# A planned attention and gated-MLP kernel: the planner groups matmuls by array mode, weight narrowing is spread differently, and the last block's first feature tile is cut in two

## The chip, the cores and the metric

The kernel runs on one NeuronCore of a Trainium2 chip. The metric is device time in microseconds (us) of one execution, with all loads from and stores to HBM. Five engines work side by side, each through its own instructions in order: PE (TensorE, matrix products; its weight loads are listed as PEld), DVE (VectorE), ACT (ScalarE), POOL (GpSimd) and SP (SyncE, which here issues the transfers).

## What is computed

Performer attention over 8 batches x 8 heads x 576 tokens x 64, with 128 random features, then RMS norm and a gated MLP on all 4608 tokens (512 to 1536 to 512). Cut to the core:

```python
def phi(x):                                   # x: q or k, scaled by 64 ** -0.25
    proj = einsum('bhsd,md->bhsm', x, omega)  # 128 features
    h = proj - sum(x * x, -1) / 2
    return exp(h - max(h, -1)) / sqrt(m)
kv, z = einsum('bhsm,bhsd->bhmd', phi(k), v), phi(k).sum(2)
num, den = einsum('bhsm,bhmd->bhsd', phi(q), kv), einsum('bhsm,bhm->bhs', phi(q), z) + 1e-6
x = (num / den) as 4608 x 512
xn = x / sqrt(mean(x * x) + 1e-6) * rms_g
g = xn @ w_gate                               # 512 x 1536, float64
out = (g * sigmoid(g) * (xn @ w_val)) @ w_out # 1536 x 512, float64
```

The three weight matrices come in as float64 and are narrowed to float32 on the chip.

## The kernel before

**Tiling.** Tokens go in 36 chunks of 128, and four chunks make a block of 512 columns (9 blocks). A product of float32 operands is made of three passes: each operand is held as a high part and a remainder, and `three_pass` multiplies high by high (L209), high by remainder (L210) and remainder by high (L211).

**Phase one** (0 to 453.6 us in the profile) makes the attention and the first 4 of the 12 feature tiles of the MLP, f0 to f3. For each chunk of k and of q, `project` (L512, a bank of pool psJ) multiplies 64 rows of the array per head, `peak` takes maxima on DVE (L525), `exps` runs on ACT (L542). `kv_mid` (L601) and `kv_half` (L640) sum keys against values, 64 columns of the array at a time. For each chunk `attend` then transposes the q features (`turn`, L673, matmuls with the identity), multiplies them with kv (`mix`, L684, 64 columns of the array), divides (`divide`, DVE L698 to L700), scales (L722), transposes (`xturn`, L734), copies to `xr` and to the high part (ACT, L740 and L750), takes the remainder on POOL (`xlo`, L753) and stores (`xstore`, L743). When the four chunks of a block are done, `gated` multiplies each feature tile: 12 matmuls of 512 columns for the gate and 12 for the value, each into a bank of pool psF (2 banks), then ACT L808, DVE L812 and L818, and the store L823. Until the first of these, the planner fills PE's idle time with `spin` (L840), a matmul of 512 columns with no use for its result.

**Phase two** (453.6 to 805 us) makes the other 8 feature tiles by products of the Strassen-Winograd kind: in each of two passes (PASSES, two tile pairs each), 5 pairs of blocks by 4 units (a unit is gate or value of a tile pair), a unit being 7 products of 6 matmuls. The products go to bank `a` (pool psJ), `b` (psM) and `c` (psF). Between them ACT copies bank contents out (`keep`, L1047) and DVE adds them (`total`, L1054). The seventh product (on Rt4) accumulates into bank `a` again, so it starts only when `total` c22 on DVE has read it. The left operands of the products (`left`, lw_0 to lw_6) are loaded and split by ACT L900 and POOL L905, the right ones (`right`, Xb loads L944) by DVE and ACT, once for a pair of blocks.

**Phase three** (805 us to the end) is the product with w_out.

**Narrowing.** `weights(n)` narrows one of 36 weight tiles: a load of float64 (L312), a scaled magnitude on ACT (L316), four passes on DVE (L322, L330, L341, L352). Tiles 0 to 7 serve f0 to f3. Tiles 8 to 23 (w_gate, w_val of phase two) and 24 to 35 (w_out) are followed by `sums` (DVE L418) and stores, to be loaded again as left operands.

**What sets the order.** Every step is an item of `Plan`, with an engine, a duration, predecessors, a key and the buffers that it takes and gives. `order` simulates the engines: whenever an engine is free it takes the ready item with the lowest key whose buffers are free. The instructions are written out in that order, and each engine then runs its own in that order. The items of a unit have keys from 6000 on (one per unit), those of phase one have lower ones. KEYS holds numbers for the first chunks and for tiles 0 to 7. Tiles 8 to 15 have keys 508 to 515, so they are taken in phase one. Tiles 16 to 35 have keys 6000.2, 6001.2 and so on, one per unit in the first pass of phase two, in buffers of group "later". The planner also holds back the consumers of a step by a slack on each engine (SLACK), and a transfer by its landing time.

## Time and profile before

| what | value |
|---|---|
| time, median of three runs (least to most) | 1080.81 us (1080.77 to 1081.55) |
| the profiled execution, its own time | 1080.16 us |
| its span, first to last instruction | 1078.4 us |
| PE busy | 1058.0 us, 98% of the span |
| DVE, ACT, POOL busy | 839.5, 655.4, 143.0 us (78%, 61%, 13%) |
| mean granted clock of TensorE | 0.995 of full speed |
| the chain that ended last, by engine | PE 47%, DVE 6%, issue 2%, DMA 1%, ACT 1% |

PE is busy nearly all the time, so what remains is in single places: the stages of rows 1 show in which stretches PE's busy time falls short of the stretch's length or the granted clock short of 1.00. A timeline then shows in brackets how long PE was idle ahead of an instruction and what released it. On a timeline the start of one matmul to the start of the next is what it costs; the "us" beside it is the time it was in the array, and overlaps the next.

### The profile page before, as it was taken

Reading aid. Unit: us, or ns where it says so; the run is one execution under the profiler, and the core shown is the slowest. Engines: PE = TensorE matmul, PEld = TensorE weight load, DVE = VectorE, ACT = ScalarE, POOL = GpSimd, SP = SyncE. Lnnn points to the kernel's source line nnn. Section 1 sums busy time; section 2 is a strip of 40 time slices with the busy share of each in tenths; the row PEclk is TensorE's granted clock in tenths of the full one; section 3 lists DMA queues with packets and bytes.
Section 4 is the critical chain, followed back from the end, with each engine's and each line's share of the span. In section 5 each row is a group of like instructions: output and inputs, shape, how many; then the busy total and the mean of one; then the engine's idle time right before and its main releaser. Section 6 shows DMA issues by size and latency. Waiting matters only on the chain.

```text
span 1078.4 us, 20580 instructions
## 1 busy us (share of the span) xinstructions
PE 1058.0 (98%) x7709; PEld 881.2 (82%) x7709; DVE 839.5 (78%) x1451; ACT 655.4 (61%) x1429; POOL 143.0 (13%) x183
## 2 busy tenths in 40 slices
PE   9999999999999999989999999999999999999998
PEld 6787888888888887868887877888898888888888
DVE  5999999867875553689999997865659997959573
ACT  7998779858976763456546557454347554444433
POOL 0223111211121121270000017000000000000000
PEclk9999999999999999999999999999999999999999
DMA  8866786655643322678775756432337837162321
GB/s 312 273 221 193 229 281 217 201 171 167 177 121 113 99 79 77 184 257 267 231 222 193 236 193 211 137 100 86 108 119 243 289 123 224 69 208 103 114 92 50
DMA packets 107172, 188.49 MB, mean 175 GB/s; under 512 B 9152, under 2 KB 51520, under 8 KB 107072
## 3 DMA queue, kind: packets, MB, share of 16 engines
q1 hardware_dynamic: 106848, 186.88, 53.8%
q8 instruction: 61, 1.00, 0.4%
q10 hardware_dynamic: 224, 0.30, 0.1%
q14 instruction: 39, 0.32, 0.1%
HBM read 127.11 MB, written 60.03 MB: 174 GB/s over the span
## 4 chain that ended last, share of the span: by engine, by line
PE 47%; DVE 6%; issue 2%; DMA 1%; ACT 1%; POOL 0%; SPq 0%; DVEq 0%; ACTq 0%
PE pa L209 5%; PE qa L210 5%; PE qa L211 5%; PE qa L209 5%; PE pa L211 4%; PE pa L210 4%; PE qb L211 2%; PE qb L209 2%; PE qb L210 2%; PE pb L209 2%; PE pb L210 2%; PE pb L211 2%; DVE c L1054 1%; PE qc L211 1%; PE qc L210 1%
## 5 line engine op out<-in xcount | busy, mean ns | idle before, releaser
L209 PE MATMUL ff<-xhi,whi 128*128 128x512 f32 x288 | 119.9, 416 | 1.4 <-ACT xhi L750 1.4
L210 PE MATMUL ff<-xlo,whi 128*128 128x512 f32 x288 | 114.1, 396 | 0.8 <-POOL xlo L753 0.8
L211 PE MATMUL ff<-xhi,wlo 128*128 128x512 f32 x288 | 114.2, 396 | 0.0
L542 ACT ACTIVATE qp<-pjq,biq 128x128 f32<-128x128 f32 x288 | 80.9, 391 | 11.6 <-DVE biq L533 11.3
L542 ACT ACTIVATE kp<-pjk,bik 128x128 f32<-128x128 f32 x272 | 75.9, 399 | 4.6 <-DVE bik L533 4.6
L753 POOL TENSOR_TENSOR xlo<-xr,xhi 128x512 fp32r<-128x512 f32 x36 | 46.3, 1286 | 194.4 <-ACT xhi L750 194.4
L209 PEld LDWEIGHTS ff<-xhi,whi 128*128 128x128 f32 x288 | 54.9, 191 | 14.2 <-ACT xhi L750 1.6
L1208 DVE TENSOR_TENSOR hb<-hb,hb 128x1024 f32<-128x1024 f32 (+1 forms) x60 | 65.8, 1113 | 0.7
L211 PEld LDWEIGHTS ff<-xhi,wlo 128*128 128x128 f32 x288 | 54.8, 190 | 12.4
L1092 ACT ACTIVATE c<-c 128x512 f32<-128x512 f32 (+1 forms) x60 | 34.8, 588 | 48.3 <-DVE c L1054 48.0
L210 PEld LDWEIGHTS ff<-xlo,whi 128*128 128x128 f32 x288 | 54.9, 191 | 10.9 <-POOL xlo L753 1.2
L525 DVE TENSOR_REDUCE mxk<-pjk 128x4 f32<-128x512 f32 x72 | 46.9, 682 | 13.0 <-PE pjk L512 13.0
L1047 ACT COPY m<-pa 128x512 f32<-128x512 f32 (+1 forms) x40 | 21.7, 542 | 54.3 <-PE pa L211 54.3
L525 DVE TENSOR_REDUCE mxq<-pjq 128x4 f32<-128x512 f32 x72 | 47.1, 682 | 5.7 <-PE pjq L512 5.2
L676 ACT COPY qpT<-qt 128x512 f32<-128x512 f32 x72 | 39.8, 598 | 19.3 <-PE qt L673 19.1
L818 DVE SCALAR_TENSOR_TENSOR h<-u,ff 128x512 f32<-128x512 f32 x36 | 24.7, 685 | 32.0 <-PE ff L211 31.7
L684 PEld LDWEIGHTS nu<-kv,qpT 128*64 128x64 f32 x1152 | 38.7, 137 | 11.3 <-issue 6.0
L684 PE MATMUL nu<-kv,qpT 128*64 128x65 f32 x1152 | 47.3, 226 | 0.3 <-DVE kv L650 0.3
L1054 DVE TENSOR_TENSOR c<-pb,u 128x512 f32<-128x512 f32 (+1 forms) x40 | 25.2, 631 | 25.0 <-PE pb L211 17.9
L673 PE MATMUL qt<-ident,qp 128*128 128x128 f32 x288 | 40.6, 276 | 3.1 <-DVE x L700 2.9
L710 ACT ACTIVATE xn<-x 128x512 f32<-128x512 f32 x36 | 23.1, 640 | 32.7 <-DVE x L700 32.7
L512 PE MATMUL pjq<-om,inq 64*128 64x128 f32 x576 | 42.2, 284 | 0.6 <-ACT qp L542 0.6
(208 smaller groups left out, 3168.4 us busy)
## 6 DMA issues: line engine op xcount, KB each, us to landing
hb<-h_scratch SPq DMA_DIRECT2D x48, 512.0 KB, 4.6
inq<-in_qx_dram SPq DMA_DIRECT2D x36, 512.0 KB, 4.2
ink<-in_kx_dram SPq DMA_DIRECT2D x34, 512.0 KB, 4.6
Xb<-xn_scratch SPq DMA_DIRECT2D x32, 512.0 KB, 5.0
h_scratch<-c SPq DMA_DIRECT2D x64, 256.0 KB, 2.5
f<-in_wgv_dram SPq DMA_DIRECT2D x24, 512.0 KB, 4.5
xn_scratch<-xr SPq DMA_DIRECT2D x36, 256.0 KB, 4.4
h_scratch<-h SPq DMA_DIRECT2D x36, 256.0 KB, 4.2
```

Of the source, the lines that this page charges most:

```text
L209: nc.tensor.matmul(out, lhsT=ah, rhs=bh, start=first, stop=False, skip_group_check=again)
L210: nc.tensor.matmul(out, lhsT=ah, rhs=bl, start=False, stop=False, skip_group_check=again)
L211: nc.tensor.matmul(out, lhsT=al, rhs=bh, start=False, stop=last, skip_group_check=again)
L512: nc.tensor.matmul(t["pts"][i][:, hp, :], lhsT=x[rows, hp, :], rhs=om[rows, :], start=hp == 0 or not first, stop=True, skip_group_check=first,
L525: ve.tensor_reduce(out=by_half[:, i, :], in_=t["pts"][i], axis=AX.X, op=ALU.max)
L542: nc.scalar.activation(st[tag + "p", c][:, h, :], t["pts"][h % 2][:, h // 2, :], AF.Exp, bias=t["bi"][:, h : h + 1], scale=SCALE,)
L673: nc.tensor.transpose(t["pt", half][:, i, :], st["qp", c][:, 4 * half + i, :], ident)
L676: nc.scalar.copy(t["qpT"][:, 4 * half : 4 * half + 4, :], t["pt", half])
L684: nc.tensor.matmul(pt[lo:hi, i, :], lhsT=t["qpT"][:, h, lo:hi], rhs=st["kv", b][:, h, :], start=True, stop=True,)
L753: nc.gpsimd.tensor_tensor(out=st["xT", blk][1][:, :, cs], in0=t["xr"], in1=st["xT", blk][0][:, :, cs].bitcast(F32), op=ALU.subtract,)
L1054: ve.tensor_tensor(out=t[name], in0=t[bank], in1=t[y], op=ALU.add)
L1208: ve.tensor_tensor(out=t[nm, g], in0=t[x, g], in1=t[y, g], op=ALU.subtract)
```

## The change

It has six parts. (1) Items of PE carry a mode: "rows" for `project`, "columns" for `kv_half` and `mix`, "full" for the rest. Among items with a key below FILL the planner takes those of the mode in force first, and it reckons SWITCH, 0.096 us, for a change of mode. Its durations for `project`, `kv_half` and `mix` are smaller by what the switch now counts. (2) The numbers of KEYS are new. (3) Tiles 8 to 23 are all narrowed in phase one, each after the value product of a feature tile (PACE: tile 8+k after number 2k-2). Tiles 24 to 35 are narrowed in the first pass of phase two, tile 24+k after the seventh product of unit int(1.25 k). (4) The four feature tiles are taken in the order in which their weights are ready by KEYS (f0, f3, f2, f1), each after the one ahead. (5) In the last block the first feature tile is made in 384 columns (of the block's first three chunks) and then in the 128 columns of the last chunk, 24 and 24 matmuls, and the four tiles take banks of psF and psJ in turn. (6) The set `prompt`: the last chunk's store, the first pair's right loads and the loads of the first unit's left operands hold nobody back by a slack, and those left operands get a key ahead of the right loads (FRONT).

```diff
+PACE = (-2, 2, 0, 1.25)
+FRONT = 0.45
+SWITCH = 0.096
+FILL = 900.0
...
                 queue.sort()
+                if eng == "PE":
+                    queue.sort(key=lambda x: x[0] >= FILL or self.items[x[1]][8] != mode)
...
+                        if eng == "PE":
+                            dur += SWITCH * (form != mode)
+                            mode = form
...
-                        when = kinds.get(self.items[u][0], 0)
+                        when = 0 if u in self.prompt else kinds.get(self.items[u][0], 0)
...
+        ws = [[st["w", f, j]] + st.get("ff", []) for j in range(2)]
+        give = [("xT", blk)] if f == last else []
+        end = blk == NBLK - 1
+        st["nth"] = st.get("nth", 0) + end
+        bank = "psF" if st["nth"] % 2 == end else "psJ"
+        if end and st["nth"] == 1:
+            cut = TB - P
+            parts = {}
+            for j in range(2):
+                after = xs[:-1] + ws[j]
+                for cc in range(NCC):
+                    after = [
+                        add("PE", 3 * (cut / 2400 + 0.0145),
+                            lambda j=j, cc=cc: ff(j, 0, cut, cc), after, key,
+                            [] if cc else [(bank, at, j)])
+                    ]
+                ws[1].extend(after) if j == 0 else None
+                parts[j] = after
+            g = add("PE", 12 * 0.067, lambda: ff(0, cut), xs + parts[0], key)
+            v = add("PE", 12 * 0.067, lambda: ff(1, cut), [g] + parts[1], key, (), give)
+        else:
+            g = add("PE", 2.73, lambda: ff(0), xs + ws[0], key, [(bank, at, 0)])
+            v = add("PE", 2.73, lambda: ff(1), [g] + ws[1], key, [(bank, at, 1)], give)
+        gates.append(v)
+        st["ff"] = [v]
...
-    for n in range(2 * FA + 4 * len(PASSES[0])):
-        weights(n, KEYS["w"][n] if n < 2 * FA else 500 + n)
+    for n in range(2 * FA):
+        weights(n, KEYS["w"][n])
     for blk in range(NBLK):
-        for f in range(FA):
+        for f in sorted(range(FA), key=lambda f: max(KEYS["w"][2 * f : 2 * f + 2])):
             gated(blk, f, 1000 + blk * FA + f)
+    for n in range(2 * FA, 2 * NF):
+        at = PACE[0] + PACE[1] * (n - 2 * FA)
+        weights(n, 500 + n, after=[gates[int(at)]] if at >= 0 else ())
...
-    for n in range(2 * FA + 4 * len(PASSES[0]), 3 * NF):
-        key = 6000.2 + SLOW * (n - 2 * FA - 4 * len(PASSES[0]))
-        weights(n, key, "L", [in_b])
...
+            for n in range(2 * NF, 3 * NF):
+                at = PACE[2] + PACE[3] * (n - 2 * NF)
+                weights(n, base - 15 + at, "L", [in_b, st["last", int(at)]])
...
-            left(ps, un, base + slot(un))
+            left(ps, un, base + slot(un) if slot(un) else base - 0.5 - FRONT)
```

Over the program, PE goes from one mode to another 214 times before the change and 199 times after it; ahead of the first feature tile 44 and 46 times. There are 57 spins before and 68 after, all ahead of the first feature tile; the other PE work ahead of that tile is the same in amount. (Line numbers of the changed kernel are higher by 11 to 49; L840 is L884 there, L684 L698.)

On PE, in the start-up, the order before has around one run of spins (`qt` are transposes of q features, `xt` those of the scaled chunk, `nu` mixes, `pjk` and `pjq` projections):

```order
L512 MATMUL pjk_0_696<-om,ink_491 128x128
L512 MATMUL pjk_1_697<-om,ink_491 128x128
L673 MATMUL qt_0_713<-ident,qp_581 128x128 x4
L673 MATMUL qt_1_722<-ident,qp_581 128x128 x4
L840 MATMUL spin<-ones 128x512 x8
L734 MATMUL xt_770<-ident,xn_719 128x128 x4
L684 MATMUL nu_0_783<-kv_471,qpT_712 64x65 x8
L512 MATMUL pjq_0_799<-om,inq_544 128x128
```

and after the change, at the corresponding place:

```order
L698 MATMUL nu_1_703<-kv_495,qpT_304 64x65 x8
L884 MATMUL spin<-ones 128x512
L687 MATMUL qt_0_719<-ident,qp_550 128x128 x4
L884 MATMUL spin<-ones 128x512 x2
L687 MATMUL qt_1_734<-ident,qp_550 128x128 x4
L884 MATMUL spin<-ones 128x512 x9
L748 MATMUL xt_792<-ident,xn_741 128x128 x4
L698 MATMUL nu_0_804<-kv_495,qpT_718 64x65 x8
```

The transposes now stand with spins between them, nine of them ahead of `xt`, and a mix stands ahead of the spins.

On PE, at the start of the last block, where `xt` is the transposition of a chunk of that block and `ff_0_0` the gate product of f0 (brackets: the engines on which the instruction waits), before:

```order
L734 MATMUL xt_6477<-ident,xn_6453 128x128 [waits DVE_49,PE_49]
L734 MATMUL xt_6477<-ident,xn_6453 128x128 x3
L209 MATMUL ff_0_0_6490<-xhi_6154,whi_150 128x512 [waits DVE_49,Activation_49]
L210 MATMUL ff_0_0_6490<-xlo_6155,whi_150 128x512 [waits Pool_49]
L211 MATMUL ff_0_0_6490<-xhi_6154,wlo_154 128x512
L209 MATMUL ff_0_0_6490<-xhi_6154,whi_150 128x512
```

and after, the start of the 384 columns:

```order
L748 MATMUL xt_6607<-ident,xn_6583 128x128 [waits DVE_49,PE_49]
L748 MATMUL xt_6607<-ident,xn_6583 128x128 x3
L220 MATMUL ff_0_0_6614<-xhi_6292,whi_150 128x384 [waits DVE_49]
L221 MATMUL ff_0_0_6614<-xlo_6293,whi_150 128x384 [waits Pool_49]
L222 MATMUL ff_0_0_6614<-xhi_6292,wlo_154 128x384
```

and where these pass over to the 128 columns:

```order
L220 MATMUL ff_0_1_6633<-xhi_6292,whi_150 128x384
L221 MATMUL ff_0_1_6633<-xlo_6293,whi_150 128x384
L222 MATMUL ff_0_1_6633<-xhi_6292,wlo_154 128x384
L220 MATMUL ff_0_0_6614<-xhi_6292,whi_150 128x128 [waits Activation_49]
L221 MATMUL ff_0_0_6614<-xlo_6293,whi_150 128x128 [waits Pool_49]
L222 MATMUL ff_0_0_6614<-xhi_6292,wlo_154 128x128
```

The waits for the last chunk's copy on ACT and remainder on POOL have moved from the first two matmuls of the tile to its 25th and 26th; the 384-column part still waits for POOL.

On DVE, in the second and third unit of phase two (`c` are the additions L1054 and the products of gate and value L1101, `mag`, `w` and `sr` the narrowing and its sums, `Xt` a difference of right operands), before:

```order
L330 TENSOR_SCALAR mag_6954<-mag_6954 128x512
L341 SCALAR_TENSOR_TENSOR w_7030<-f_17_6905,mag_6954 128x512
L352 SCALAR_TENSOR_TENSOR w_7030<-f_17_6905,w_7030 128x512
L957 TENSOR_TENSOR Xt_1_7046<-Xb_1_6757,Xt_1_6942 128x1024
L1101 TENSOR_TENSOR c_0_1_7060<-pa_1_6897,c_0_0_6907 128x512
L322 TENSOR_SCALAR mag_7043<-mag_7043 128x512
L330 TENSOR_SCALAR mag_7043<-mag_7043 128x512
L341 SCALAR_TENSOR_TENSOR w_7075<-f_18_6993,mag_7043 128x512
L1054 TENSOR_TENSOR c_0_2_7083<-pb_2_7032,u_0_2_7069 128x512
L352 SCALAR_TENSOR_TENSOR w_7075<-f_18_6993,w_7075 128x512
L418 TENSOR_TENSOR sr_7097<-w_7075 128x256
L1054 TENSOR_TENSOR c_0_2_7102<-pa_2_6998,m_0_2_7055 128x512
```

and after:

```order
L1102 TENSOR_TENSOR c_0_1_7178<-pc_1_7149,m_0_1_7088 128x512
L1150 TENSOR_TENSOR c_0_1_7178<-c_0_1_7178,c_0_0_7058 128x512
L352 SCALAR_TENSOR_TENSOR w_7195<-f_24_7097,mag_7147 128x512
L363 SCALAR_TENSOR_TENSOR w_7195<-f_24_7097,w_7195 128x512
L1150 TENSOR_TENSOR c_0_1_7214<-pa_1_7066,c_0_0_7073 128x512
L1102 TENSOR_TENSOR c_0_2_7244<-pb_2_7200,u_0_2_7231 128x512
L333 TENSOR_SCALAR mag_7246<-mag_7246 128x512
L341 TENSOR_SCALAR mag_7246<-mag_7246 128x512
L1102 TENSOR_TENSOR c_0_2_7260<-pa_2_7182,m_0_2_7222 128x512
```

Two of a tile's passes at a time stand between these additions after the change, where the passes of two tiles and a first sum stood before.

## Rows read from the trace of the kernel before

**Rows 1.** Windows: length, busy (count) PE, PEld, DVE, ACT, POOL, clock, DMA, GB/s.

```profile
0.00:69.50 69.50, 66.57 (x857) 52.23 (x857) 56.85 (x137) 59.06 (x169) 14.60 (x27) 1.00 0.84 280
69.50:110.00 40.50, 37.71 (x338) 30.91 (x335) 37.98 (x90) 36.69 (x102) 13.19 (x16) 0.96 0.63 200
110.00:427.00 317.00, 316.77 (x3480) 266.25 (x3479) 230.64 (x568) 226.88 (x638) 57.05 (x84) 1.00 0.52 160
427.00:453.60 26.60, 24.39 (x101) 19.61 (x100) 12.97 (x14) 11.18 (x18) 2.71 (x3) 0.94 0.64 193
453.60:500.00 46.40, 42.09 (x176) 33.58 (x175) 41.31 (x55) 29.44 (x57) 28.27 (x27) 0.96 0.79 246
500.00:615.00 115.00, 114.36 (x501) 92.53 (x500) 112.44 (x180) 60.48 (x96) 0.00 (x0) 1.00 0.70 227
615.00:665.00 50.00, 46.01 (x267) 38.98 (x266) 45.32 (x63) 30.50 (x70) 22.00 (x22) 1.00 0.62 207
```

**Rows 2.** Timeline of PE, start-up, nine spins: start, us, instruction, count.

```profile
21.52 2.73 PE L840 MATMUL spin<-ones 128*128 128x512 f32 x9
```

**Rows 3.** Timeline of PE, two mixes alone, then two together, each with its next.

```profile
50.13 0.69 PE L684 MATMUL nu<-kv,qpT 128*64 128x65 f32 x16
50.75 1.16 PE L512 MATMUL pjk<-om,ink 64*128 64x128 f32 x16
...
59.89 1.15 PE L684 MATMUL nu<-kv,qpT 128*64 128x65 f32 x32
60.97 0.73 PE L840 MATMUL spin<-ones 128*128 128x512 f32 x2
```

**Rows 4.** Timeline of PE, 93 to 97 us; in brackets idle time and releaser.

```profile
94.13 0.63 PE L673 MATMUL qt<-ident,qp 128*128 128x128 f32 x4 [0.75 <-DVE x L700]
96.06 0.63 PE L673 MATMUL qt<-ident,qp 128*128 128x128 f32 x4 [1.30 <-DVE x L700]
```

**Rows 5.** Timeline of PE, last block of phase one, and phase two's first product.

```profile
428.99 0.50 PE L209 MATMUL ff<-xhi,whi 128*128 128x512 f32 x1 [1.37 <-ACT xhi L750]
430.34 0.50 PE L210 MATMUL ff<-xlo,whi 128*128 128x512 f32 x1 [0.85 <-POOL xlo L753]
...
431.16 0.52 PE L210 MATMUL ff<-xlo,whi 128*128 128x512 f32 x1
...
434.46 0.50 PE L209 MATMUL ff<-xhi,whi 128*128 128x512 f32 x1
...
453.64 0.39 PE L209 MATMUL pa<-Rb11h,lw_0h 128*128 128x512 f32 x1
```

**Rows 6.** One stretch of 1 us, columns as in Rows 1.

```profile
433.00:434.00 1.00, 1.00 (x3) 0.74 (x3) 0.00 (x0) 0.00 (x0) 0.00 (x0) 0.50 0.74 274
```

**Rows 7.** Timeline of PE, 256-column products, and transposes between full-array matmuls.

```profile
628.86 0.28 PE L209 MATMUL pb<-Rt1h,lw_3h 128*128 128x256 f32 x1
...
630.18 0.28 PE L211 MATMUL pa<-Rt2h,lw_4l 128*128 128x256 f32 x1
...
112.81 0.60 PE L673 MATMUL qt<-ident,qp 128*128 128x128 f32 x4
113.16 0.48 PE L209 MATMUL ff<-xhi,whi 128*128 128x512 f32 x1
```

**Rows 8.** Timeline of PE, phase two's first units.

```profile
463.35 0.50 PE L209 MATMUL pa<-Rt4h,lw_2h 128*128 128x512 f32 x1 [1.35 <-DVE c L1054]
486.01 0.79 PE L209 MATMUL pa<-Rt4h,lw_2h 128*128 128x512 f32 x1 [2.09 <-DVE c L1054]
```

**Rows 9.** Timeline of DVE, a weight tile's four narrowing passes begin, and their successor.

```profile
567.66 0.42 DVE L322 TENSOR_SCALAR mag<-mag 128x512 f32<-128x512 f32 x1
569.91 1.22 DVE L905 TENSOR_TENSOR Rb11l<-Xb,Rb11h 128x1024 fp32r<-128x1024 f32 x1
```

**Rows 10.** Timeline of PE, two waits around the first pass's end.

```profile
644.79 0.50 PE L210 MATMUL pb<-Rb22l,lw_6h 128*128 128x512 f32 x1 [0.84 <-DVE Rb22l L905]
649.76 0.50 PE L209 MATMUL pa<-Rb11h,lw_0h 128*128 128x512 f32 x1 [0.79 <-ACT lw_0h L900]
```

More of the change, by code (lines that the diff above doesn't have):

```diff
@@ L120, in __init__, with add @@
         self.until = None
[L122 to L123 removed]
+        self.prompt = set()
+    def add(self, eng, dur, fn, after=(), key=0.0, take=(), give=(), land=0.0, mode="full"):
+        self.items.append((eng, dur, fn, tuple(after), key, tuple(take), tuple(give), land, mode))
         return len(self.items) - 1
@@ L658, in kv_half @@
         ps = ("psM", "kvp", b, half)
-        m = add("PE", 2.05, heads, after, key, [ps], give)
+        m = add("PE", 1.86, heads, after, key, [ps], give, mode="columns")
         st["kvh", b, half, "pe"] = m
@@ L774, in attend @@
             give = ([("qpT", c)] + [("kv", b) for b in ends]) if half else []
-            i = add("PE", 0.7, lambda h=half: mix(h), after, key - 0.2,
-                    [ps] if half else [ps, ("x", c)], give)
+            i = add("PE", 0.48, lambda h=half: mix(h), after, key - 0.2,
+                    [ps] if half else [ps, ("x", c)], give, mode="columns")
             mixed = [i]
```

57 lines of the change are left out of this document (34 added, 23 removed).

## The prediction

> **What bounds the kernel now.** I read the stages first, then the timeline of PE where a stage falls short. PE is busy in 114.36 of 115 us from 500 to 615 us and in 316.77 of 317 from 110 to 427 [rows 1], so in the long stretches the end is set by how many matmuls there are and how closely they follow each other. Five stretches fall short. From 0 to 69.5 PE is idle for 2.93 us, from 69.5 to 110 for 2.79, from 427 to 453.6 for 2.21, from 453.6 to 500 for 4.31, and from 500 to 665 for 0.64 + 3.99 [rows 1]. In three of them the granted clock is 0.96, 0.94 and 0.96 [rows 1]. The waits are of few kinds. At 94 and 96 us PE waits for DVE's division [rows 4]. In the last block it waits 1.37 us for the copy and 0.85 us for the remainder of the last chunk [rows 5]. In phase two it waits 1.35 and 2.09 us for an addition on DVE before a seventh product [rows 8], and around the end of the first pass for a remainder (0.84) and a cast (0.79) of operands [rows 10].
>
> Behind the last block's wait the clock drops: in the microsecond from 433 it is 0.50, the lower level of 1.2 GHz [rows 6]. Eight matmuls start from 431.16 to 434.46, 3.30 us, and the 84 after them take (453.64 - 434.46) / 84 = 0.2283 us each [rows 5]; eight at that pace are 1.83 us, so the drop costs 1.47. The clock of the stretches from 69.5 and from 453.6 (0.04 missing of 40.5 and 46.4 us, 1.6 and 1.9) says that each holds one such spell, behind about 2 us of waiting; I take 1.5 for each.
>
> **The change part by part**, against the profiled execution's 1080.16 us. Its span is 1078.4; the 1.76 around it stays. The median of the runs, 1080.81, is 0.65 higher, which is added at the end.
>
> *A. Mode switches, 214 to 199.* Two mixes each by itself take 50.75 - 50.13 = 0.62 us until the next begins, two together 60.97 - 59.89 = 1.08 [rows 3]. So a switch costs 2 x 0.62 - 1.08 = 0.16, and 15 fewer give -2.4. The ends: nothing, if the 0.16 is a weight load that shows anyway, and -4.1 at 0.27, the 0.50 us in the array of a 512-column matmul beyond its 0.2283 [rows 5]; the middle value is the only row with the switch in it. The Trainium skill, "TensorEngine Tiling (Array Packing)", section "Key Properties", says that a change of mode drains TensorE. If each switch emptied the array the term would be -4.1 instead of -2.4; the trace's 0.16 speaks for less than that.
>
> *B. Start-up.* The planner writes 11 more spins ahead of the first feature tile; the other work ahead of it is the same. Nine spins take 2.73 us [rows 2], 0.30 each, so +3.3. Of the 2.93 us that PE was idle there [rows 1] some is covered by spins now, as they stand in front of transposes that wait; a quarter, 0.7, gives +2.6. All of it covered would be +0.4; I take +1.9 for the near end, since part of that idle time is before anything is loaded. The far end, +5, is a start-up in which the reordered keys add waits that no row shows.
>
> *C. 81 to 110 us.* Here stand 2.79 us of waiting and the 1.5 of the clock. The waits are for divisions and the two mixes behind them [rows 4], and all four feature tiles are now in the order in which their weights are ready, with other keys around them. I keep 1.1 of the 4.29, so -3.2 (ends -4.3 and -2).
>
> *D. The last block.* The 384 columns need the first three chunks only, and 24 matmuls of them cover the last chunk's chain. A 512-column product follows at 0.2283 [rows 5], a 256-column one at (630.18 - 628.86) / 11 = 0.12 [rows 7], so one of 384 at the mean, 0.174, and 24 are 4.2 us: more than the 2.22 of the wait. That takes away 2.22 and the 1.47 of the clock. The price is 24 more matmuls. Transposes with 128 columns start every (113.16 - 112.81) / 4 = 0.0875 us [rows 7], the nearest row, which gives 24 x (0.174 + 0.0875 - 0.2283) = +0.8; the line through 256 and 512 columns gives 0.066 and +0.3, and no more than the 256-column pace gives +1.6. Sum -2.9 (-3.4 to -2.1). If the cover were gone, 2.2 of waiting would be back and the 0.8 lost. The Trainium skill, "TensorE: Matmul & The Clock Gate", section "LDWEIGHTS (loading the stationary operand)", makes a weight load its columns over 1.2 GHz, an estimated 0.107 us for 128, which a 128-column piece could not go below. By it the split would cost 24 x (0.174 + 0.107 - 0.2283) = +1.3 and the sum would be -2.4; the transposes at 0.0875, with 128 columns of weights too, speak against it.
>
> *E. Start of phase two.* The waits at 463.35 and 486.01 are for additions of DVE [rows 8], and DVE is busy in 41.31 of 46.4 us there and 112.44 of 115 after [rows 1]. An addition that is ready stands behind narrowing passes in DVE's order; the change leaves one tile's passes between the additions of the second and third unit where two tiles' passes and sums stood. A tile's four passes take 569.91 - 567.66 = 2.25 us [rows 9], and a seventh product has the sixth's 6 x 0.2283 = 1.4 us as cover, so two tiles can't hide and one may almost. First units' left operands come in front of the right loads now; they hide behind the last block's 19 us of matmuls. Of 4.31 + 1.5 = 5.8 I keep 1.1: -4.7 (-5.8 to -2).
>
> *F. 500 to 665 us.* Pass one narrows 12 tiles instead of 20, 18 us less for a DVE that is busy for 199 of these 211 us [rows 1]. Idle 4.63; I keep the remainder and the cast, 1.6 [rows 10], which are no additions: -3.0 (-4.6 to -1.4).
>
> *G. Phase one gets the 8 tiles*, 18 us of DVE and eight loads, and each load now waits on SP for a feature tile's product; the stores of x and h stand behind it. From 110 to 427 DVE is busy for 230.64 of 317 us, ACT for 226.88, the DMA share is 0.52 [rows 1]: there is room of 86 us. But `divide` and `silu` share the queue, and PE waits if a two-us group lands in front of one. I take +1.0 (0 to +4).
>
> Sum: -2.4 + 2.6 - 3.2 - 2.9 - 4.7 - 3.0 + 1.0 = -12.6, so 1067.6 for the profiled execution and **1068.2** for the median. If the ends fall independently the sum moves by some 4 down and 6 up: 1064 to 1074.
>
> **Rivals.**
> *R1, the waits move.* Removing a wait lets PE run on to the next late step; two of the three spells (about 2.2 of waiting and 1.5 of clock each) appear elsewhere in phase one. For it: nearly all of KEYS is new, and DVE is 94% busy from 69.5 to 110 [rows 1]. Against it: the room from 110 on. 1068.2 + 2 x 3.7 = about 1076.
> *R2, the additions are late by themselves*, not through the narrowing (ACT's copy, then DVE, then PE). Then E and F stay: 1068.2 + 7.7 = about 1076. Against it: the long stretch with only 0.64 idle has the same chain in all its units [rows 1].
> *R3, slower: the start-up.* DVE is busy for 56.85 and ACT for 59.06 of the first 69.5 us [rows 1]. If the new keys put the first block's divisions behind k-feature maxima and weight narrowing, the first feature tile slides, and everything behind it with it. The savings without B are 15.2, so it decides once the first feature tile starts more than 15 us later than 69.5, beyond about 84.7; at 87 the time is about 1083. Against it: the planner has 11 spins more, 3.3 us, not 15.
> *R4, the cut does nothing.* The 384 columns wait on POOL for the third chunk; if that ends as late as the last chunk did, D turns from -2.9 to +0.8: about 1072. For it: POOL's remainders queue one after the other.
>
> **How the numbers follow.** Forecast 0.64, R1 0.14, R2 0.10, R3 0.07, R4 0.05. What a measurement of this kernel can tell from no change is about 0.2%, 2.2 us. The forecast and R4 are faster; of R1 and R2, at 4.8 us below the median, 0.16 is faster and 0.08 within; R3 is slower: 0.85, 0.08, 0.07. The range is 1061 to 1077: its upper end takes in R1, R2 and R4, its lower end has the good ends of A to F fall together, 6.7 more. What is left out is R3 and the tails, 0.2 at most.
>
> **What would show it.** A: `mix` and `project` in longer runs, total PE busy down. B: 68 spins and a first feature tile at about 72 us; past 76 B is wrong. C and D: clock 1.00 from 69.5 to 110 and in the last block; no wait between `xt` and the 384 columns or before the 128, and these at 0.07 to 0.11 us. E: no wait over 1 us before a seventh product up to 500 us. F: DVE under 95% from 500 to 615. G: PE idle under 1 us in the middle of phase one. The forecast is wrong if PE's idle time in total, some 20 us now, stays above 12, or if spells at 0.50 are seen at other places.

## The result, and the profile after

The changed kernel takes 1067.88 us (median of four runs, 1066.81 to 1069.53), against 1080.79 us before in the same comparison: a ratio of 0.9881, interval 0.9866 to 0.9896, so 12.9 us or 1.2% faster. The profiled execution took 1067.79 us with a span of 1066.0, 12.4 us less than before.

The sum came out at almost the forecast number. Where the time went is another matter, and three marks on PE's timeline tell it: the first matmul of a feature tile, the first product of phase two, and the first product of the second pass. The view of windows, cut at these marks and at the end of the last block's `xt`, gives for the kernel before (columns as in [rows 1]):

```profile
0.00:69.53 69.53, 66.60 (x858) 52.23 (x858) 56.88 (x137) 59.06 (x169) 14.63 (x27) 1.00 0.84 280
69.53:427.62 358.09, 355.08 (x3820) 297.51 (x3816) 268.99 (x658) 263.56 (x738) 70.21 (x100) 1.00 0.53 164
427.62:453.64 26.02, 23.81 (x97) 19.26 (x97) 12.61 (x14) 11.20 (x18) 2.75 (x3) 0.93 0.65 197
453.64:649.76 196.12, 187.47 (x877) 153.33 (x875) 187.29 (x285) 108.31 (x191) 35.02 (x34) 0.99 0.70 227
649.76:1078.40 428.64, 425.08 (x2064) 358.86 (x2064) 313.74 (x361) 213.25 (x314) 20.36 (x21) 1.00 0.43 141
```

and for the changed kernel:

```profile
0.00:74.19 74.19, 70.30 (x868) 54.88 (x869) 59.74 (x145) 60.39 (x175) 15.54 (x27) 1.00 0.80 270
74.19:425.30 351.11, 349.70 (x3817) 295.26 (x3816) 291.09 (x698) 265.03 (x741) 70.82 (x100) 1.00 0.59 188
425.30:448.60 23.30, 23.30 (x123) 20.47 (x122) 13.28 (x14) 11.53 (x19) 8.13 (x8) 1.00 0.79 253
448.60:637.26 188.66, 184.72 (x878) 152.37 (x876) 162.95 (x237) 103.82 (x182) 27.65 (x29) 1.00 0.59 190
637.26:1066.00 428.74, 425.34 (x2064) 358.93 (x2064) 313.82 (x361) 213.11 (x314) 20.35 (x21) 1.00 0.43 141
```

Read the lengths: start-up +4.66, the middle of phase one -6.98, the last block -2.72, the first pass of phase two -7.46, the rest +0.10. In the last block PE is busy in all of its 23.30 us where 2.21 were idle, and in the first pass DVE is busy for 24 us less. The same window as the sixth of [rows 1] shows DVE at 97.69 of 115 us, 85% where it was 98%:

```profile
500.00:615.00 115.00, 114.44 (x535) 94.88 (x534) 97.69 (x155) 59.41 (x101) 5.64 (x7) 1.00 0.55 178
```

The last block on PE's timeline, to be held against [rows 5]:

```profile
424.95 0.60 PE L748 MATMUL xt<-ident,xn 128*128 128x128 f32 x4
425.30 0.42 PE L220 MATMUL ff<-xhi,whi 128*128 128x384 f32 x1
...
429.57 0.22 PE L220 MATMUL ff<-xhi,whi 128*128 128x128 f32 x1
429.63 0.28 PE L221 MATMUL ff<-xlo,whi 128*128 128x128 f32 x1
...
432.08 0.28 PE L222 MATMUL ff<-xhi,wlo 128*128 128x128 f32 x1
...
448.60 0.39 PE L220 MATMUL pa<-Rb11h,lw_0h 128*128 128x512 f32 x1
```

There is no bracket of idle time. The 24 wide matmuls go from 425.30 to 429.57, 0.178 us each (0.173 once they follow each other), and the narrow ones from 429.63 to 432.08 are 22 steps of 0.111. What still waits in phase two:

```profile
457.51 0.50 PE L220 MATMUL pa<-Rt4h,lw_2h 128*128 128x512 f32 x1 [0.58 <-DVE c L1102]
479.71 0.50 PE L220 MATMUL pa<-Rt4h,lw_2h 128*128 128x512 f32 x1 [1.04 <-DVE c L1102]
...
637.26 0.50 PE L220 MATMUL pa<-Rb11h,lw_0h 128*128 128x512 f32 x1 [0.72 <-ACT lw_0h L944]
```

The waits of [rows 8] are down to 0.58 and 1.04 us, and no spell at 0.50 is left: the granted clock of every window above is 1.00. Of the two waits in [rows 10], the one for a cast at the start of the second pass, 0.79, is 0.72, and the one for a remainder, 0.84, is 1.04 at 632.38.

### The profile page after: what moved, and what is told of

Same layout as the page of the kernel before. It is cut to its first block, busy times and chain, and to the rows that moved or that the text cites. A ratio compares the mean times of both kernels' runs of the same rounds, so it can differ in the third digit from the quotient of the medians.

```text
span 1066.0 us, 20634 instructions
## 1 busy us (share of the span) xinstructions
PE 1053.4 (99%) x7744; PEld 881.9 (83%) x7744; DVE 840.9 (79%) x1451; ACT 653.9 (61%) x1429; POOL 142.5 (13%) x183
## 4 chain that ended last, share of the span: by engine, by line
PE 86%; DVE 8%; issue 2%; DMA 2%; ACT 1%; POOL 1%; SPq 0%; DVEq 0%; ACTq 0%; POOLq 0%
PE ff L220 6%; PE ff L222 6%; PE ff L221 6%; PE pa L220 5%; PE pa L222 5%; PE pa L221 5%; PE qa L221 5%; PE qa L220 5%; PE qa L222 5%; PE nu L698 3%; PE pjq L523 3%; PE pjk L523 3%; PE kvp L654 3%; PE qt L687 3%; PE pb L220 2%; PE pb L221 2%
## 5 line engine op out<-in xcount | busy, mean ns | idle before, releaser
L220 PE MATMUL ff<-xhi,whi 128*128 128x512 f32 (+2 forms) x296 | 120.6, 407 | 0.0
L222 PE MATMUL ff<-xhi,wlo 128*128 128x512 f32 (+2 forms) x296 | 114.7, 388 | 0.1
L221 PE MATMUL ff<-xlo,whi 128*128 128x512 f32 (+2 forms) x296 | 114.6, 387 | 0.0
L698 PEld LDWEIGHTS nu<-kv,qpT 128*64 128x64 f32 x1152 | 38.7, 137 | 11.3 <-issue 6.7
L698 PE MATMUL nu<-kv,qpT 128*64 128x65 f32 x1152 | 47.0, 226 | 0.0
L1150 DVE TENSOR_TENSOR c<-c,c 128x512 f32<-128x512 f32 (+1 forms) x60 | 40.8, 686 | 1.8
L523 PE MATMUL pjk<-om,ink 64*128 64x128 f32 x576 | 40.6, 282 | 0.0
```

What stands on the lines that cost most here:

```text
L220: nc.tensor.matmul(out, lhsT=ah, rhs=bh, start=first, stop=False, skip_group_check=again)
L221: nc.tensor.matmul(out, lhsT=ah, rhs=bl, start=False, stop=False, skip_group_check=again)
L222: nc.tensor.matmul(out, lhsT=al, rhs=bh, start=False, stop=last, skip_group_check=again)
L523: nc.tensor.matmul(t["pts"][i][:, hp, :], lhsT=x[rows, hp, :], rhs=om[rows, :], start=hp == 0 or not first, stop=True, skip_group_check=first,
L698: nc.tensor.matmul(pt[lo:hi, i, :], lhsT=t["qpT"][:, h, lo:hi], rhs=st["kv", b][:, h, :], start=True, stop=True,)
L1150: ve.tensor_tensor(out=t[nm], in0=t[src], in1=g[nm], op=ALU.mult)
```

## The experiments

Twelve kernels ran. The table has the marks of one profiled execution of each; the time from the first feature tile to phase two's first product is "phase one", from there to the second pass's first product "pass one". The first mark alone moves by up to 1.3 us (73.5 to 74.8) between the nine kernels here that have the same start-up on PE as the changed one. The kernel before took 1079.05 to 1080.79 us in the four comparisons from which the medians come, so a ratio to it, given with its interval, says more than the difference of two medians.

| kernel | first feature tile at | phase one | pass one | rest | span | median us |
|---|---|---|---|---|---|---|
| before | 69.5 | 384.1 | 196.1 | 428.6 | 1078.4 | 1080.8 |
| changed | 74.2 | 374.4 | 188.7 | 428.7 | 1066.0 | 1067.9 |
| x1_uncut | 74.8 | 377.4 | 186.4 | 428.8 | 1067.3 | 1067.7 |
| x2_cut256 | 73.7 | 373.3 | 190.2 | 429.0 | 1066.1 | 1066.8 |
| x3_64s | 73.5 | 378.7 | 188.9 | 428.2 | 1069.3 | 1071.1 (one run) |
| x4_old_pace | 74.5 | 375.3 | 192.6 | 428.4 | 1070.8 | 1072.7 |
| x5_pace_alone | 70.6 | 388.7 | 189.0 | 428.2 | 1076.4 | 1078.2 |
| x6_no_modes | 71.3 | 385.0 | 188.8 | 428.2 | 1073.3 | 1077.8 |
| x8_no_front | 74.2 | 376.0 | 193.4 | 428.4 | 1072.0 | 1073.7 |
| x9_old_keys | 74.3 | 377.5 | 191.5 | 428.1 | 1071.4 | 1073.4 |
| x11_half_spins | 75.8 | 376.3 | 188.7 | 428.5 | 1069.3 | 1070.9 |
| x12_late_pace | 73.6 | 374.8 | 191.3 | 434.0 | 1073.7 | 1075.3 |
| x13_256_late | 74.0 | 373.6 | 191.8 | 434.1 | 1073.5 | 1073.6 |
| x15_256_ungated | 74.4 | 373.3 | 190.9 | 428.4 | 1067.0 | 1068.8 |

### The cut of the last block

**x1_uncut**, the tile in one piece again:

```diff
-        if end and st["nth"] == 1:
+        if end and st["nth"] == 99:
```

> The changed kernel with the last block's first feature tile in one piece of 512 columns again (12 + 12 matmuls instead of 24 + 24); the banks still alternate. Theory: the cut removed a wait for the last chunk's chain and the half-clock spell behind it, at the price of 24 matmuls of 128 columns. Undone, the 2.2 us of waiting and about 1.5 us of the clock come back and 24 x (0.173 + 0.111 - 0.228) = 1.3 us go: +2.4 us, about 1070.2 us, with a granted clock of 0.50 behind the wait. Rival: the new order brings the last chunk in time anyway, the wait does not come back and the kernel gains the 1.3 us: about 1066.6 us.

The stretch did what the theory said, and the total did not: 1067.74 us, ratio to before 0.9882 (0.9866 to 0.9899), the same as with the cut. On PE's timeline the waits are back in their old size, the window of two microseconds behind them is at 0.50, and phase one is 3.0 us longer:

```profile
427.46 0.50 PE L220 MATMUL ff<-xhi,whi 128*128 128x512 f32 x1 [1.37 <-ACT xhi L764]
428.81 0.50 PE L221 MATMUL ff<-xlo,whi 128*128 128x512 f32 x1 [0.84 <-POOL xlo L767]
...
471.71 0.50 PE L220 MATMUL pa<-Rt4h,lw_2h 128*128 128x512 f32 x1 [0.38 <-DVE c L1102]
```

```profile
430.00:432.00 2.00, 2.00 (x7) 1.52 (x6) 0.00 (x0) 0.00 (x0) 0.00 (x0) 0.50 0.86 251
```

But the waits at the seventh products are now one of 0.38 us instead of 0.58, 1.04 and 0.48, and pass one is 2.3 us shorter; these waits are 1.7 of it. DVE's timeline of the changed kernel shows how the first of them comes about. The first remainder of the right operands, Rb11l, stands directly behind the second feature tile's product of gate and value (L840), which waits for PE, and from there DVE works nearly without a break until the additions at 456:

```profile
437.92 0.69 DVE L840 SCALAR_TENSOR_TENSOR h<-u,ff 128x512 f32<-128x512 f32 x1 [1.40 <-PE ff L222]
438.52 1.56 DVE L949 TENSOR_TENSOR Rb11l<-Xb,Rb11h 128x1024 fp32r<-128x1024 f32 x1
...
454.50 1.76 DVE L949 TENSOR_TENSOR Rt4l<-Xt,Rt4h 128x1024 fp32r<-128x1024 f32 x1
456.18 0.68 DVE L1102 TENSOR_TENSOR c<-pb,u 128x512 f32<-128x512 f32 x1
```

So this chain goes with the feature tiles. Its last remainder for the first unit, Rt4l, starts 454.50 - 448.60 = 5.90 us behind phase two's first product. It does so too in x3 (below), whose last block, from `xt` to that product, is 4.3 us longer (27.95 us instead of 23.65): 458.08 - 452.18 = 5.90. The waits there are 0.59, 1.78 and 0.47, so it is not the shorter block that makes them.

```profile
441.49 0.69 DVE L840 SCALAR_TENSOR_TENSOR h<-u,ff 128x512 f32<-128x512 f32 x1 [1.43 <-PE ff L222]
442.10 1.53 DVE L949 TENSOR_TENSOR Rb11l<-Xb,Rb11h 128x1024 fp32r<-128x1024 f32 x1
...
458.08 1.76 DVE L949 TENSOR_TENSOR Rt4l<-Xt,Rt4h 128x1024 fp32r<-128x1024 f32 x1
```

```profile
452.18 0.39 PE L220 MATMUL pa<-Rb11h,lw_0h 128*128 128x512 f32 x1
```

What differs in the uncut kernel is the order that the planner wrote. ACT casts the first unit's left operands behind the first feature tile's gate (from 433.57), not behind the second's (435.69 in the changed kernel), and on DVE Rb11l stands ahead of the second tile's product. Rt4l starts 456.19 - 452.12 = 4.07 us behind the first product:

```profile
440.29 1.23 DVE L949 TENSOR_TENSOR Rb11l<-Xb,Rb11h 128x1024 fp32r<-128x1024 f32 x1 [0.25 <-ACT Rb11h L944]
441.44 0.69 DVE L840 SCALAR_TENSOR_TENSOR h<-u,ff 128x512 f32<-128x512 f32 x1
...
456.19 1.21 DVE L949 TENSOR_TENSOR Rt4l<-Xt,Rt4h 128x1024 fp32r<-128x1024 f32 x1
```

```profile
452.12 0.39 PE L220 MATMUL pa<-Rb11h,lw_0h 128*128 128x512 f32 x1
```

The second wait has a like cause: in the changed kernel a narrowing pass that waits 1.91 us for its magnitude stands on DVE ahead of the addition at 478.97 (its rows stand under x15); in the uncut kernel the same addition, at 478.84, stands ahead of the pass, at 481.01. No run has the cut together with the uncut kernel's order.

**x2_cut256**, 256 and 256 columns instead of 384 and 128:

```diff
-            cut = TB - P
+            cut = TB // 2
...
-                after = xs[:-1] + ws[j]
+                after = xs[: cut // P] + ws[j]
...
```

(The planner's duration for the second part is 12 x 0.12 instead of 12 x 0.067 us, here and in x13 and x15.)

> The changed kernel with that tile cut in 256 and 256 columns; the first part waits for the first two chunks of the block only. Theory: a piece of 128 columns costs 0.111 us, nearly what one of 256 costs (0.12), so the narrow piece wastes its weight loads: 24 x (0.12 + 0.12) = 5.76 us instead of 24 x (0.173 + 0.111) = 6.82 us, 1.06 us less, about 1066.8 us, as 24 x 0.12 = 2.9 us still cover the 2.2 us of the last chunk's chain. Rival: the cover of 2.9 us is too short once the waits for the copy and the remainder come with their own delays; 0.3 to 1 us of waiting comes back and the time is 1067.9 or more.

Phase one is 1.1 us shorter, as expected, with no wait in the last block. Pass one is 1.5 us longer: the wait for an addition at 478.84 grew to 1.96 us and a half-clock spell stands behind it. Rt4l again starts 5.90 us behind the first product and the first wait is 0.59; what grew is ACT's wait for the load of a narrowing, 4.48 us where it was 3.58, which holds DVE ahead of that addition. The median, 1066.78 us (0.9878, 0.9863 to 0.9892), can't be told from the changed kernel's.

**x3_64s**, the narrow part in 64 and 64 columns:

```diff
-            g = add("PE", 12 * 0.067, lambda: ff(0, cut), xs + parts[0], key)
+            g = add("PE", 12 * 0.067, lambda: (ff(0, cut, cut + 64), ff(0, cut + 64)), xs + parts[0], key)
```

(and the same for the value product).

> The changed kernel with the 128 columns of the last block's first tile made as 64 and 64 columns: 48 narrow matmuls instead of 24. In the changed kernel 128 columns took 0.111 us each. Theory: a narrow matmul is bound by the load of its 128 weight columns, so one of 64 columns takes 0.11 us too and the part goes from 2.7 to about 5.3 us. Rival: its time goes with the columns that move and a fixed part, so 64 columns take some 0.06 to 0.08 us and the part stays within 3 to 4 us. The rows of these matmuls decide, not the total, which is 1068 to 1071 us by either.

A matmul of 64 columns takes as long as one of 128: the 45 steps below are (434.01 - 428.98) / 45 = 0.112 us each.

```profile
428.98 0.28 PE L222 MATMUL ff<-xhi,wlo 128*128 128x64 f32 x1
...
434.01 0.28 PE L222 MATMUL ff<-xhi,wlo 128*128 128x64 f32 x1
434.12 0.47 PE L220 MATMUL ff<-xhi,whi 128*128 128x512 f32 x1
```

So the count of moving columns does not set it. The weight loads do, as far as the rows go: they have 128 columns here as there, and PEld is busy in all 5.03 us of these steps; no run changed their columns. The Trainium skill, "TensorE: Matmul & The Clock Gate", section "LDWEIGHTS (loading the stationary operand)", gives a weight load its columns over 1.2 GHz, an estimated 0.107 us for 128, and the trace agrees with 0.111 and 0.112. The section on the hardware below comes back to the clock behind these matmuls.

### The narrowing of the weights

**x4_old_pace**, the changed kernel with the old places:

```diff
-    for n in range(2 * FA, 2 * NF):
-        at = PACE[0] + PACE[1] * (n - 2 * FA)
-        weights(n, 500 + n, after=[gates[int(at)]] if at >= 0 else ())
+    for n in range(2 * FA, 2 * FA + 4 * len(PASSES[0])):
+        weights(n, 500 + n)
...
+    for n in range(2 * FA + 4 * len(PASSES[0]), 3 * NF):
+        key = 6000.2 + 1.0 * (n - 2 * FA - 4 * len(PASSES[0]))
+        weights(n, key, "L", [in_b])
...
-            for n in range(2 * NF, 3 * NF):
-                at = PACE[2] + PACE[3] * (n - 2 * NF)
-                weights(n, base - 15 + at, "L", [in_b, st["last", int(at)]])
```

> The changed kernel with the weights narrowed where they were before: tiles 8 to 15 in phase one without waits for feature tiles, tiles 16 to 35 in the first pass of phase two, one per unit; all else as changed. Theory: narrowing on DVE ahead of additions makes PE's waits in phase two, so the 448.6 to 637.3 us stretch (188.7 us) gets back to about 196 us: +7.5 us, about 1075.4 us, with a half-clock spell near the start of phase two. Rival (the additions are late by themselves and the loads in front did it): no more than +1 us, about 1068.5 us.

Between the two: 1072.70 us (0.9932, 0.9917 to 0.9947), pass one 3.9 us longer, half of the 7.46. A wait of 2.05 us for an addition at 470.52 and a spell behind it are back.

**x5_pace_alone**, the kernel before with the new places only:

```diff
-    for n in range(2 * FA + 4 * len(PASSES[0])):
-        weights(n, KEYS["w"][n] if n < 2 * FA else 500 + n)
+    for n in range(2 * FA):
+        weights(n, KEYS["w"][n])
...
+    for n in range(2 * FA, 2 * NF):
+        at = PACE[0] + PACE[1] * (n - 2 * FA)
+        weights(n, 500 + n, after=[gates[int(at)]] if at >= 0 else ())
...
+                weights(n, base - 15 + at, "L", [in_b, st["last", int(at)]])
```

> The kernel before with the new places of the narrowing alone (tiles 8 to 23 in phase one, 24 to 35 paced in phase two's first pass). Theory, from the changed kernel with the old places (+3.9 us in the stretch from phase two's first product to the second pass, +0.8 in phase one): the stretch of 196.1 us shortens by about 4, phase one stays within 1 us, about 1076.5 us. The prediction's terms E, F and G for this part alone: -7.7 + 1.0, about 1074 us. Rival: phase one has no room for eight more tiles without the new order, its waits grow, and the time is 1080 us or more.

Pass one shortens by 7.2 us, nearly the whole of E and F, but phase one grows by 4.6, and the median is 1078.22 us: ratio 0.9992 (0.9982 to 1.0002), no difference. In phase one there is a new wait for the last chunk's scaling, ahead of the two old ones:

```profile
431.40 0.63 PE L734 MATMUL xt<-ident,xn 128*128 128x128 f32 x4 [1.54 <-DVE xn L722]
433.40 0.50 PE L209 MATMUL ff<-xhi,whi 128*128 128x512 f32 x1 [1.37 <-ACT xhi L750]
434.74 0.80 PE L210 MATMUL ff<-xlo,whi 128*128 128x512 f32 x1 [0.84 <-POOL xlo L753]
```

and the changes of mode behind the first feature tile are 186 instead of 170. So the eight tiles in phase one do cost something where PE's order is not grouped; in x4, where it is, taking them out again did not shorten phase one (375.3 against 374.4).

**x12_late_pace**, the tiles of w_out five units later:

```diff
-PACE = (-2, 2, 0, 1.25)
+PACE = (-2, 2, 5, 1.1)
```

> The changed kernel with the 12 narrowings of w_out started five units later and a little closer (PACE third and fourth number 5 and 1.1 instead of 0 and 1.25). In the changed kernel PE still waits for additions at 457.5 (0.58 us), 479.7 (1.04) and 508.0 (0.48), and at 478.17 DVE stood idle for 1.91 us because a narrowing pass ahead of the addition waited for its magnitude from ACT. Theory: it is the narrowing in front of the addition, by its load more than by its time on DVE, so the waits at 479.7 and 508.0 go and the one at 457.5, ahead of which only right operands stand, stays: 1.5 us less, about 1066.4 us. Rival: DVE's work for the right operands makes all three, they stay, and the time is within 0.5 us of 1067.9.

The waits at 479.7 and 508.0 are gone and the one at 457 stays at 0.58, as the theory had it. The total is 1075.29 us (0.9948, 0.9934 to 0.9963): the last tiles were not ready at the end of the pass. DVE ends the last sums of the narrowing at 639.6 us, in the changed kernel at 597.5.

```profile
614.58 0.58 PE L220 MATMUL pa<-Rt4h,lw_2h 128*128 128x256 f32 x1 [2.12 <-DVE c L1102]
639.71 0.80 PE L220 MATMUL pa<-Rb11h,lw_0h 128*128 128x512 f32 x1 [4.03 <-DMA Xb<-xn_scratch]
...
645.30 0.79 PE L220 MATMUL pa<-Rt4h,lw_2h 128*128 128x512 f32 x1 [1.89 <-DVE c L1102]
```

Three waits of 2.12, 4.03 and 1.89 us, and the granted clock of the window from 640 to 660 us was 0.78. That price was not in either expectation.

**x13_256_late**, this and the cut at 256 together:

```diff
-PACE = (-2, 2, 0, 1.25)
+PACE = (-2, 2, 5, 1.1)
...
-            cut = TB - P
+            cut = TB // 2
...
```

> The cut in 256 and 256 columns and the later narrowing of w_out together. With the cut alone the first product of phase two came 1.1 us sooner after the first feature tile (373.3 instead of 374.4 us), and a longer wait for an addition (1.96 us) and a half-clock spell gave it back. Theory: the longer wait stood behind a narrowing, so with the later narrowing the cut's 1.1 us is kept: about 1065.3 us, with no spell at 0.50. Rival: phase two's first units are bound by DVE's work for the right operands, which takes the 1.1 us again: about 1066.4 us or more.

1073.62 us (0.9936, 0.9921 to 0.9951), with the same waits at the end of the pass (2.11, 4.52, 1.89), which hide what the run was made for.

**x15_256_ungated**, the cut at 256 and the loads of w_out not held to a unit:

```diff
-                weights(n, base - 15 + at, "L", [in_b, st["last", int(at)]])
+                weights(n, base - 15 + at, "L", [in_b])
```

> The cut in 256 and 256 columns (1066.8 us) and the narrowings of w_out with the same keys but without waiting for a unit, so their loads are issued as soon as a buffer is free. Started five units later they took away the waits at 479.7 and 508.0 us but were late at the end of the pass (4.0 us there). Theory: a narrowing pass that waits on DVE for its load holds the addition behind it; with loads early the wait of 1.96 us at 478.8 and the half-clock spell behind it (1.5) go and the end of the pass stays as it was: 2 to 3.5 us less, 1063.5 to 1065 us. Rival: it is the time of the passes on DVE and not their load; the wait stays or moves, 1066.5 us or more.

This theory fell. In the changed kernel DVE had stood still for the load of a narrowing, by way of ACT:

```profile
478.17 0.43 DVE L333 TENSOR_SCALAR mag<-mag 128x512 f32<-128x512 f32 x1 [1.91 <-ACT mag L327]
...
478.97 0.68 DVE L1102 TENSOR_TENSOR c<-pa,m 128x512 f32<-128x512 f32 x1
```

With the loads let go, 1068.78 us (0.9904, 0.9889 to 0.9919): the waits at 457 and 479 are there, 0.59 and 1.49, and new ones of 1.58 us for ACT's copy at 472.37 and of 0.68 at 519.06. The edit did not take the load away: the first one is issued 15.8 us behind the first product as before, the second 5.6 us sooner than that, and ACT still waits for loads, 4.17, 1.40 and 2.71 us ahead of three magnitudes up to 478 us. But ahead of the addition behind the wait at 479.62 DVE has no idle time; narrowing passes and sums fill it from 475.38 to 478. It is not the load alone. With x12 together: that a narrowing stands in the first units makes the two later waits, whether by its load or by its time on ACT and DVE; the first, at 457, belongs to the right operands. In the uncut kernel (x1) the same narrowings, in another order, leave one wait of 0.38.

### Modes, numbers and fronts

**x6_no_modes**, without the second sort of PE's queue:

```diff
-                if eng == "PE":
-                    queue.sort(key=lambda x: x[0] >= FILL or self.items[x[1]][8] != mode)
```

> The changed kernel without the second sort of PE's queue, so that the planner does not look for items of the mode in force; it still reckons 0.096 us for a change of mode. Changes of mode rise by 21 (222 instead of 201 by the same count), 67 spins instead of 68. Theory: one change costs 0.10 to 0.16 us, so +2.1 to +3.4 us, about 1070.0 to 1071.3 us. If each emptied the array at 0.27 us: +5.7 us, about 1073.6 us. Rival: the changes hide in weight loads, and what PE gained between the first feature tile and the last block is the order's: within 0.5 us, about 1068 us.

1077.82 us (0.9977, 0.9965 to 0.9990), 10 us above the changed kernel, more than any of the three expected. Phase one is 10.6 us longer, while the first feature tile comes 2.9 us sooner. Of the 10.6, 3.1 are idle time: the last chunk is late again, this time behind the 384 columns and ahead of the narrow part:

```profile
432.69 0.33 PE L218 MATMUL ff<-xhi,whi 128*128 128x128 f32 x1 [1.37 <-ACT xhi L762]
434.04 0.33 PE L219 MATMUL ff<-xlo,whi 128*128 128x128 f32 x1 [1.01 <-POOL xlo L765]
```

```profile
434.00:440.00 6.00, 5.96 (x28) 5.58 (x29) 1.37 (x2) 0.60 (x1) 0.00 (x0) 0.59 0.68 204
440.00:442.00 2.00, 2.00 (x7) 1.57 (x6) 0.00 (x0) 0.00 (x0) 0.00 (x0) 0.53 0.94 242
```

The clock that is missing in these windows, 0.41 of 6 us and 0.47 of 2, is by estimate worth 3.4 us. The remaining 4.0 stand beside 21 more changes of mode behind the first feature tile (174 against 153), 0.19 us each.

**x9_old_keys**, the old numbers in KEYS:

```diff
-    "k": [-33.3, -25.2, -18.0, -12.8, -12.3, -11.3, -1.5, -1.2, 2.2],
-    "q": [-31.0, -5.0, -3.9, -3.1, 3.9, 4.8, 5.0, 6.6, 8.3],
+    "k": [-34.0, -29.2, -15.1, -14.2, -13.2, -12.7, -2.5, -0.7, 0.9],
+    "q": [-29.3, -4.1, -4.0, -2.2, 3.9, 4.6, 4.9, 6.0, 8.4],
...
-    "attend": -28.75,
+    "attend": -19.12,
```

> The changed kernel with the old numbers of KEYS. 191 changes of mode instead of 201, 73 spins instead of 68. Spins half as long did not bring the first feature tile sooner (75.8 us instead of 74.2), so the order of the start-up sets it. Theory: the new numbers start the first feature tile later by 4.7 us and pay by fewer waits behind it; with the old ones it starts near 69.5 to 71 us, the waits for divisions between 80 and 100 us (2 to 2.8 us) and a half-clock spell (1.5) come back: 1066 to 1068 us, no difference. Rival: the numbers fit the sorting by mode only, the first blocks wait longer, and the time is 1071 us or more.

The rival's number: 1073.36 us (0.9952, 0.9935 to 0.9968). The first feature tile did not come sooner (74.3). Phase one is 3.1 us longer by seven waits of 0.3 to 1 us, and pass one 2.8 us by a wait of 3.11 us for an addition at 484.44.

**x11_half_spins**, spins of 256 columns:

```diff
-        nc.tensor.matmul(pt, lhsT=ones[:, :P], rhs=ones, start=True, stop=True)
+        nc.tensor.matmul(pt[:, : DM // 2], lhsT=ones[:, :P], rhs=ones[:, : DM // 2], start=True, stop=True)
```

> The changed kernel with spins of 256 columns instead of 512, in the same 68 places, so PE has some 68 x 0.11 = 7.5 us less of them to do ahead of the first feature tile. Theory: the start-up is bound by DVE and ACT, spins only fill, and the first feature tile starts within 1 us of 74.2. Rival (the prediction's term for the start-up): spins push the work behind them, 0.30 us each; then the first feature tile comes up to 7 us sooner, at 67 to 70 us, and the time falls to about 1062 us if the clock stays at full speed.

The first feature tile starts at 75.8 us, later by 1.6 and not sooner by up to 7. PE is idle for 75.80 - 69.46 = 6.3 us up to there instead of 3.9. The spins fill; they don't push. The total is 1070.88 us (0.9908, 0.9892 to 0.9925), slower. Of the 1.9 us that phase one behind it lost, 1.6 are two new waits, 1.27 for a scaling on DVE at 81.92 and 0.33 for a copy on ACT at 119.99; why these come is open.

**x8_no_front**, without part 6:

```diff
-                        when = 0 if u in self.prompt else kinds.get(self.items[u][0], 0)
+                        when = kinds.get(self.items[u][0], 0)
...
-            left(ps, un, base + slot(un) if slot(un) else base - 0.5 - FRONT)
+            left(ps, un, base + slot(un))
```

> The changed kernel without part 6: the last chunk's store and the first loads of phase two hold their users back by the slack again, and the first unit's left operands come behind the right loads. Theory: this part made the other half of what phase two gained (the old places of the narrowing alone gave back 3.9 of 7.5 us), so +2 to +3.6 us, about 1070 to 1071.5 us, with waits at the first products. Rival: 16 us of the last block's matmuls hide these loads in either order; within 0.7 us, about 1068 us.

1073.68 us (0.9956, 0.9941 to 0.9971), above the changed kernel by 5.8 us by the medians and by 8 by the ratios, and more than the theory's upper end. The first product waits for its left operand, the third for its remainder on POOL, and then an addition is late:

```profile
450.21 0.50 PE L220 MATMUL pa<-Rb11h,lw_0h 128*128 128x512 f32 x1 [1.25 <-ACT lw_0h L944]
451.88 0.55 PE L222 MATMUL pa<-Rb11h,lw_0l 128*128 128x512 f32 x1 [0.94 <-POOL lw_0l L949]
...
475.87 0.63 PE L220 MATMUL pa<-Rt4h,lw_2h 128*128 128x512 f32 x1 [3.28 <-DVE c L1102]
```

A clock of 0.52 stands behind the 3.28 us.

## Why the prediction was right, and where it was not

The forecast was 1068.2 us and the time is 1067.88. The terms, against the marks:

| term | forecast | measured |
|---|---|---|
| B, start-up | +2.6 | +4.66 |
| A, C and G, middle of phase one | -2.4 - 3.2 + 1.0 = -4.6 | -6.98 |
| D, last block | -2.9 | -2.72 |
| E and F, pass one | -7.7 | -7.46 |

**B had the wrong mechanism.** It priced eleven spins. Halving all spins brought the first feature tile no sooner (x11), and with 67 spins, ten more than before, it starts at 71.3 us where there is no sorting by mode (x6). What moved it is the sorting: without it the tile starts at 71.3 us (x6) or 70.6 (x5, old numbers as well), with it at 73.5 to 74.8, with the old numbers at 74.3 (x9). The planner takes an item of the mode in force ahead of one with a lower key, and PE then waits more: it is idle for 3.89 us ahead of the tile, in x6 for 1.70. Some 3 us belong to the sort. What the new numbers add (71.3 against 69.5 and 70.6, where there is no sort) isn't clear of what the mark moves by itself.

**A was sized too small.** From [rows 3] a change of mode costs 0.16 us. In the middle of phase one, 1.6 us of the 6.98 are less idle time (3.01 to 1.41 by the windows) and 1.5 the spell behind 96 us; that leaves 3.9 for 17 changes fewer, 0.23 each, and x6 gave 0.19. Both prices are what is left over when waits and clock are taken off, and x9 does not show them: with five changes fewer PE is busy for 0.2 us less in phase one. By 0.23 for 15 the term is -3.5, between the value taken and the far end, -4.1. The sentence of the Trainium skill, "TensorEngine Tiling (Array Packing)", section "Key Properties", that a change of mode drains TensorE had pointed that way; no run here shows whether the array is emptied in full. I had taken one pair of mixes for a price that the middle of phase one, with all kinds of changes, shows better. What the sort saves beyond that is the last chunk's time: in x6 the 384 columns no longer covered it.

**C** was right in its mechanism: the waits of [rows 4] and the spell are gone; one wait of 1.34 us at 107.52 is left, about the 1.1 that was kept. The old numbers brought back waits of up to 1 us (x9).

**D was right in its stretch and wrong as a term of the sum.** Its price was mis-sized: a narrow matmul takes 0.111 us, so the cut costs 24 x (0.173 + 0.111 - 0.228) = 1.3 us, not 0.8. I had taken the transposes of [rows 7] at 0.0875 for the nearest row and set aside the Trainium skill's weight load of 0.107; x3 measured 0.112 and bears out the latter. The step that failed is the adding: x1 shows 3.0 us less in phase one with the cut and 2.3 us more in pass one, and no difference in the total that can be told. "Sum" assumed that what the last block saves reaches the end. But the cut also changed the order that the planner writes for ACT and DVE at the border: the right operands of the first unit come 1.8 us later against the first product (5.90 instead of 4.07), and a narrowing comes ahead of an addition. I priced each stretch by itself and not what the plan does to the next one.

**E and F** came out within 0.3 us, in part by luck, as the cut takes 2.3 us of them (x1) that no term foresaw; without it pass one is 9.7 us shorter than before, beyond the 7.7 of the forecast. The mechanism holds: fewer narrowing passes, DVE at 85% instead of 98% from 500 to 615, and with none in the first five units two of three waits are gone (x12). Not to be divided: the old places cost 3.9 us of pass one, the missing fronts 4.7, the old numbers 2.8, together more than the 7.46, as each makes the same additions late. The sentence that the left operands' loads "hide behind the last block's 19 us of matmuls" needs part 6 in the changed kernel: without it they do not (x8, 1.25 and 0.94 us), though in the kernel before, without that part, the first product did not wait [rows 5].

**G** was +1.0 for eight more tiles in phase one. In the changed kernel it is nothing that can be seen (x4). In the order before it takes part in 4.6 us (x5), beyond the far end of 4.

Of the rivals, **R1** did not come: no spell is left. **R2** was right for one wait, at 457.51, which with the cut stays under all paces and stands behind right operands alone. **R3**: the start-up was 4.7 us longer, far from the 15 that it needed. **R4**: the 384 columns begin without a wait, so the cut does what it says; that it is worth nothing to the total has the other cause.

Two of the signs named ahead came out against the prediction, by a little. PE's idle time in total, by the windows, is 3.89 + 1.41 + 0 + 3.94 + 3.40 = 12.6 us, above the 12 that were to make the forecast wrong: the start-up's grew by 1.0 where 0.7 was to go. And E's "no wait over 1 us" is missed by the 1.04 at 479.71.

The total agrees so well by luck, because two errors cancel: start-up 2.1 us dearer, the middle of phase one 2.4 us cheaper. The kernels with one part alone show how far it could have been: the narrowing by itself made no difference in the order before.

## What to carry to other kernels

Price a step in its own stretch first, and then look at the order on the other engines at the border to the next: where a planner writes all orders at once, a change of one engine's steps can move work on the others, and what it saves in one stretch can be lost in the next, as with the cut here. Parts that remove the same kind of wait (narrowing in front of additions, loads in front, the start numbers) don't add up, and one alone can be worth nothing; leaving the narrowing's places out of the finished kernel (x4) showed more here than adding them to the old one (x5). A piece of 128 columns took nearly as long as one of 256 (0.111 against 0.12 us), so two halves were cheaper than a wide and a narrow piece (x2, 1.1 us less in phase one).
